# Twelve weight halves on GpSimd, one ring of five buffers, and new transfer figures in the planner of an attention and maxout kernel

## The chip, the core and the metric

The kernel runs on one core of a Trainium2 chip. Its engines are named as in the profile: PE multiplies matrices, DVE, ACT and POOL (GpSimd) work elementwise, SP issues most transfers. The metric is the device time of one execution in microseconds (us); lower is better.

## What is computed

Causal attention over 8 batches of 8 heads (576 positions, head size 64) with a bias from cumulative sums, then an expert layer with three up projections, their maximum, and one down projection, over all 4608 tokens of width 512 (inner width 768).

```python
scores = scale * np.matmul(q, k.transpose(0, 1, 3, 2))
cum = np.cumsum(np.maximum(s, 0.0), axis=-1)
bias = -(cum[:, :, :, None] - cum[:, :, None, :])
scores = np.where(causal, -1000000000.0, scores + np.minimum(bias, 0.0))
attn = softmax(scores)
x = (attn @ v).transpose(0, 2, 1, 3).reshape(B * S, H * D)
h = np.maximum(np.maximum(x @ w1, x @ w2), x @ w3)
out = h @ w_out
```

## The kernel before

**Who sets the order.** The kernel writes no fixed order. It adds each piece of work to a list with `add`: on which engines it may run, with planned durations in ns, a priority key, what it reads and writes. The class `Plan` then runs a small model of the five queues (SP, POOL, DVE, ACT, PE): at each moment each free engine takes the ready piece with the lowest key, and an operation that two engines can do goes to the one that takes it first. The instructions are written out in that order, and each engine of the chip executes its own queue in order. So a changed planned duration costs nothing itself; it moves rows. `load` (L316) plans a transfer with its issue time, bytes by rate, and a latency until it has landed.

**Buffers.** Each kind of buffer is a ring with a depth from the table at L248. A new use of a ring of n waits until the n-th last use has been read by all its readers. Those that matter here: `m`, three PSUM buffers for results of PE; `m1`, three SBUF buffers for the running maximum of the up projections; `o`, two for the outputs on their way to memory.

**Weights.** There are 24 weight tiles of 128 x 512 elements, `w0` to `w17` for the up projections and `w18` to `w23` for the down projection, loaded as eight-byte numbers (`raw`, or `early` for some) in seven groups: three tiles each for up, all six together for down. ACT (L485), POOL (L499, `top`) and DVE (L506, `join`) turn each into fp32. PE forms a small gram block of the group (L527), DVE reduces it (L540) into `ws`, and `power` spreads the largest value over all partitions: a DVE scaling (L425), one matrix multiplication (L434, "m<-identb,ws" in the profile), a DVE maximum (L442). From it come scales: `sws` (L547 to L557), for the down group `rels` (L577). With the scale ready, the high half of a tile is written in fp16 by ACT (L599; POOL has an alternative at L603, for tiles in the range HIP), and the low half, what fp16 left over, by DVE (L637). `power` is used for the values' scales `vs` too.

**Attention.** Scores (`s`, L1149, and L1030 for pairs), masks on POOL (L1222), DVE and ACT for the softmax (L1235, L1244, L1280, L1288), transposes of the probabilities by DMA issued from SP (L1299, L1107, L1116) or for the first units on PE (turns, L1324, copied to `pT` at L1334 and L1336), then probabilities by values (`av`, L1384), whose results become `x` (L1411 to L1429).

**The expert layer.** The tokens go in 16 sets, one of 256 and one of 320 positions in each batch. Set 0 is computed in plain fp32 (`u_plain` L659, `d_plain` L689), while the scales of the weights aren't all there; it needs only raw weights. Sets 1 to 15 use the fp16 halves, three products for each: 18 up blocks `u` of 12 matrix multiplications (L1479), and four down blocks `d` of 18 (L1535). The first of three up blocks is copied from PSUM into `m1` (L1490 on ACT, L1494 on DVE), the other two are folded in by DVE's maximum (L1502); ACT writes the high half `h` (L1509), POOL its low half (L1514), the last reader of that `m1`. Each `d` block is scaled into an `o` buffer by ACT (L1554), and SP issues its transfer to memory (L1560). A set of the middle stretch of the program is worked beside the attention of the next; at the end only expert sets are left.

Of the kernel before, what the change touches and what calls it, by code (L numbers as in the profile page):

```python
# [71 lines left out]
class Plan:  # L72
# [48 lines left out]
    def run(self):  # L121
# [16 lines left out]
        while left:  # L138
# [4 lines left out]
            while events and events[0][0] <= now:  # L143
                _, _, _, op = heapq.heappop(events)
                if op is not None and op.start is None:
                    op.due = now + HOLD[0]
                    for e in op.ways:
                        heapq.heappush(wait[e], (op.key, op.n, op))
            for e in engines:
                if free[e] > now:  # L150
                    continue
                aside, pick, kept = [], None, None
                while wait[e]:
# [16 lines left out]
                if pick is None:  # L170
                    pick = kept
# [8 lines left out]
                if len(op.ways[e]) > 2:  # L180
                    dma[e] = max(dma[e], now + busy) + op.ways[e][2]
# [32 lines left out]
def kernel(  # L214
# [34 lines left out]
        qr=2, qh=2, ql=2, rv=4, vv=2, bias=2, p=2, pr=2, tl=2, pT0=2, pT1=2, tT=2, t=5, m1=3, o=2,  # L249
        sc=6, dg=2, am=3, vs=5, ws=3, os=4, s=2, av=1, m=3,  # L250
# [113 lines left out]
    def spans(c0, c1):  # L364
# [56 lines left out]
    def power(t, key):  # L421


        def do(e):
# [20 lines left out]


# [14 lines left out]

    def weights(c):
        ids = chunks[c]
        raw = {}
# [126 lines left out]
        for i in ids:  # L591
# [51 lines left out]

    def first_set(c, raw):
# [4 lines left out]
        if c < NFT:  # L649
# [3 lines left out]
            for i in range(3):  # L653
                pm = buf("m", free=True, name=f"u_plain_{c}_{i}")
                r = raw[3 * c + i]

                def up(e, r=r, pm=pm):
                    for kt in range(NKT):
                        nc.tensor.matmul(  # L659
                            pm()[:, :nq], lhsT=words(r)[0][:, kt * P:(kt + 1) * P], rhs=xb()[:, kt * nq:(kt + 1) * nq],  # L660
# [967 lines left out]
```

## Time and profile before

| what | value |
|---|---|
| median of three runs | 785.98 us (785.86 to 788.97) |
| the profiled execution | 784.61 us, span 782.6 us |
| PE busy | 764.8 us, 98% of the span |
| DVE, ACT, POOL busy | 573.8, 519.2, 308.3 us |
| moved to and from memory | 75.64 MB read, 9.58 MB written |

The span runs from the first to the last instruction that the profiler recorded; 2.0 us of the execution lie around it. An engine's busy time counts its own instructions. PEld are the weight loads of PE, which overlap its multiplications. In a timeline row stand the start, the duration, the engine, the line of the program and what is written from what; a bracket at its end gives how long the engine stood idle before it and which instruction or transfer ended that. The profile numbers buffers of one kind alike: "o" is any output buffer, "m" any of the small PSUM results.

### The profile page before, as it was taken

What the parts mean: (1) busy time and instruction counts of PE and PEld (TensorE: products, weight loads), DVE (VectorE), ACT (ScalarE), POOL (GpSimd) and SP (SyncE); (2) the same over time, 40 slices, a digit from 0 to 9 for tenths busy, and PEclk for the clock granted to TensorE, in tenths of its full rate; (3) what the DMA queues carried; (4) which work ended last, traced back from release to release, by engine and by line L of the source; (5) the groups of instructions that cost most, each with busy time, mean ns of one, the idle gap of its engine ahead of it and who ended that gap; (6) DMA issues with size and microseconds to landing.
All of it is one profiled execution on the core that took longest, in us unless ns stands there. A gap on an engine that the chain in (4) does not pass through costs nothing. (4 is left out here: it accounts for less than half of the span.)

```text
span 782.6 us, 19630 instructions
## 1 busy us (share of the span) xinstructions
PE 764.8 (98%) x7189; PEld 589.6 (75%) x7189; DVE 573.8 (73%) x1691; ACT 519.2 (66%) x1369; POOL 308.3 (39%) x361
## 2 busy tenths in 40 slices
PE   7889999999999999999999899999999999999998
PEld 5677888888888877766788677667776777778875
DVE  6999898875587888888878787888787977322131
ACT  6878777871687787986887777777876977111101
POOL 4432423641355455444544364354444452011110
PEclk9999999999999999999999999999999999999999
DMA  9799778890399899998999999898989865300000
GB/s 342 245 260 242 180 169 164 176 237 18 97 207 233 199 175 214 227 215 200 225 232 207 183 192 240 241 190 198 254 210 169 208 137 100 81 1 34 28 2 34
DMA packets 241167, 136.31 MB, mean 174 GB/s; under 512 B 204080, under 2 KB 222000, under 8 KB 241072
## 3 DMA queue, kind: packets, MB, share of 16 engines
q1 hardware_dynamic: 240912, 134.78, 75.7%
q8 instruction: 56, 0.92, 0.5%
q14 instruction: 39, 0.32, 0.2%
q10 hardware_dynamic: 160, 0.30, 0.1%
HBM read 75.64 MB, written 9.58 MB: 109 GB/s over the span
## 5 line engine op out<-in xcount | busy, mean ns | idle before, releaser
L1479 PE MATMUL u<-x,w 128*128 128x320 f16 (+1 forms) x3240 | 411.3, 287 | 2.9 <-ACT o L1554 2.9
L1479 PEld LDWEIGHTS <-w 128*128 128x128 f16 x3240 | 312.6, 98 | 99.5 <-issue 17.6
L1514 POOL TENSOR_TENSOR h<-m,h 128x320 f16<-128x320 f32 (+1 forms) x90 | 69.9, 777 | 190.4 <-ACT h L1509 174.5
L1535 PE MATMUL d<-h,w 128*128 128x320 f16 (+1 forms) x1080 | 137.9, 287 | 0.1
L1502 DVE SCALAR_TENSOR_TENSOR m<-u,m 128x320 f32<-128x320 f32 (+1 forms) x180 | 82.2, 457 | 64.3 <-PE u L1479 60.1
L1535 PEld LDWEIGHTS <-w 128*128 128x128 f16 x1080 | 104.7, 98 | 30.4 <-issue 3.2
L1222 POOL TENSOR_SCALAR_AFFINE_SELECT p<-bias 128x256 f32<-128x256 f32 (+3 forms) x91 | 68.9, 770 | 120.6 <-DVE pr L1288 68.9
L1244 ACT ACTIVATE p<-p,sc 128x256 f32<-128x256 f32 (+3 forms) x182 | 98.2, 540 | 26.3 <-DVE sc L1235 25.6
L1509 ACT ACTIVATE h<-m 128x320 f16<-128x320 f32 (+1 forms) x90 | 39.4, 438 | 102.9 <-DVE m L1502 102.6
L1288 DVE SCALAR_TENSOR_TENSOR pr<-p,sc,pr 128x256 f16<-128x256 f32 (+3 forms) x182 | 100.3, 567 | 8.0 <-ACT pr L1280 7.8
L1280 ACT ACTIVATE pr<-p,sc 128x256 f16<-128x256 f32 (+3 forms) x182 | 89.3, 538 | 13.0 <-DMA pT<-pr 7.9
L961 POOL TENSOR_TENSOR ql<-qr,qh 128x256 fp32r<-128x256 f32 (+1 forms) x76 | 82.5, 1106 | 35.0 <-ACT qh L949 30.6
L1235 DVE CUSTOM_DVE_ANT_0 p<-s,p 128x256 f32<-128x256 f32 (+3 forms) x182 | 80.4, 467 | 3.7 <-POOL p L1222 2.2
L1384 PEld LDWEIGHTS <-vv 128*64 128x64 f16 x1232 | 58.6, 110 | 18.1 <-issue 10.0
L1384 PE MATMUL av<-pT,vv 128*64 128x320 f16 (+3 forms) x1104 | 70.3, 276 | 1.2 <-DVE x L1429 0.8
L1494 DVE TENSOR_SCALAR m<-u 128x320 f32<-128x320 f32 (+1 forms) x55 | 25.3, 461 | 48.2 <-PE u L1479 47.6
L1554 ACT ACTIVATE o<-d,os 128x320 f32<-128x320 f32 (+1 forms) x60 | 28.2, 498 | 47.6 <-PE d L1535 36.8
L766 DVE TENSOR_REDUCE am<-rv 128x1 f32<-128x640 f32 (+1 forms) x44 | 33.9, 777 | 13.2 <-DMA rv<-in_qkv_dram 13.0
L1222 POOL TENSOR_SCALAR_AFFINE_SELECT ha<-bias 128x1024 f32<-128x1024 f32 (+3 forms) x29 | 26.7, 926 | 41.8 <-DVE r L1288 29.8
L1244 ACT ACTIVATE ha<-ha,sc 128x512 f32<-128x512 f32 (+3 forms) x58 | 35.9, 620 | 6.5 <-DVE sc L1235 6.1
L815 DVE SCALAR_TENSOR_TENSOR vv<-rv,vs,vv 128x640 f16<-128x640 f32 (+1 forms) x44 | 39.0, 887 | 0.4
L1288 DVE SCALAR_TENSOR_TENSOR r<-ha,sc,r 128x512 f16<-128x512 f32 (+3 forms) x58 | 37.5, 660 | 2.3 <-ACT r L1280 2.2
(170 smaller groups left out, 980.1 us busy)
## 6 DMA issues: line engine op xcount, KB each, us to landing
bias<-cd SPq DMA_DIRECT2D x32, 576.0 KB, 5.0
qr<-in_qkv_dram SPq DMA_DIRECT2D x28, 480.0 KB, 5.2
rv<-in_qkv_dram SPq DMA_DIRECT2D x32, 320.0 KB, 3.8
raw<-in_w_dram SPq DMA_DIRECT2D x16, 512.0 KB, 5.7
qr<-in_qkv_dram SPq DMA_DIRECT2D x13, 512.0 KB, 6.3
bias<-cd SPq DMA_DIRECT2D x12, 512.0 KB, 5.4
out_dram<-o SPq DMA_DIRECT2D x32, 160.0 KB, 2.4
early<-in_w_dram SPq DMA_DIRECT2D x8, 512.0 KB, 7.0
```

What stands on the lines that cost most here:

```text
L961: lambda e, d0=d0, d1=d1: E[e].tensor_tensor(out=lo().bitcast(F32R)[:, d0:d1], in0=raw()[:, d0:d1], in1=hi()[:, d0:d1], op=ALU.subtract),
L1222: nc.gpsimd.affine_select(out=pt()[:, 0:8 * P].rearrange("p (j n) -> p j n", j=2)[:, :, at:at + nk], in_=r["bias"]()[:, 2 * a * w:2 * (a + ...
L1235: lambda e, j=j: nc.vector.tensor_tensor_reduce(out=pj(j), in0=src(j), in1=pj(j) if masked else bias(j), scale=-SCALE, scalar=3.0e38, op0= ...
L1244: lambda e, j=j: nc.scalar.activation(out=pj(j), in_=pj(j), func=AF.Exp, scale=-1.0, bias=nm()[:, j:j + 1], accum_out=sm()[:, j:j + 1]),
L1280: lambda e, h_=h_, s_=s_, j=j: nc.scalar.activation(out=h_(), in_=s_(), func=AF.Copy, scale=ri()[:, j:j + 1]),
L1288: lambda e, h_=h_, l_=l_, s_=s_, j=j: nc.vector.scalar_tensor_tensor(out=l_(), in0=s_(), scalar=ri()[:, j:j + 1], in1=h_(), op0=ALU.mult, ...
L1384: nc.tensor.matmul(av()[j * D:(j + 1) * D, c0:nq], lhsT=lt, rhs=rt, start=(n < 2), stop=(n >= len(todo) - 2), skip_group_check=True,)
L1479: nc.tensor.matmul(pm()[:, :nq], lhsT=v[:, wt, kt, :], rhs=x(xt, kt), start=(k == 0), stop=(k == 3 * NKT - 1),)
L1502: lambda e, pm=pm, m1=m1: nc.vector.scalar_tensor_tensor(out=m1()[:, :nq], in0=pm()[:, :nq], scalar=HSC, in1=m1()[:, :nq], op0=ALU.mult, o ...
L1509: lambda e, m1=m1, ft=ft: nc.scalar.activation(out=h(0, ft), in_=m1()[:, :nq], func=AF.Copy),
L1514: lambda e, m1=m1, ft=ft: E[e].tensor_tensor(out=h(1, ft), in0=m1()[:, :nq], in1=h(0, ft), op=ALU.subtract),
L1535: nc.tensor.matmul(pm()[:, :nq], lhsT=v[:, wt, dt, :], rhs=h(c, ft), start=(k == 0), stop=(k == 3 * NFT - 1), skip_group_check=True,)
```

## The change

Four things change at the constants that are set (many other lines of the diff are switches that are off, or move the down part of a set into the function `down_all` as it was).

1. HIP goes from (0, 0) to (12, 24): the high halves of tiles 12 to 23 are planned on POOL alone (1300 ns), with the tensor_scalar that was there before, and no longer on ACT.
2. The rings `m1` of three and `o` of two become one ring `m1` of five; outputs take their buffers from it. The memory used is the same.
3. The figures of transfers change: a rate, a time from issue to the start of the transfer (`lead`, which takes the place of the issue time there), shorter issue times for some, and a latency with a reserve of 1500 ns on top (SPARE). The planned time of the matrix multiplication in `power` falls from 250 to 90 ns, that of the turns from 350 to 270.
4. The rule by which PE's queue is picked is written anew, with a limit on how many pieces are held back; the number of held pieces is 2.

```diff
-HOLD = (3000.0, 30000.0)
+HOLD = (3000.0, 30000.0, 2)
+SAME = 0
+SPARE = 1500.0
-HIP = (0, 0)
+HIP = (12, 24)
...
-                aside, pick, kept = [], None, None
+                aside, pick, kept = [], None, []
...
-                    if kept is not None and op.mode:
-                        break
-                    if e == "PE" and op.mode and not shape and op.due > now > HOLD[1]:
-                        kept = op
+                    if e == "PE" and op.mode:
+                        kept.append(op)
+                        if shape and (op.mode == shape or not SAME):
+                            pick = op
+                            break
+                        if not shape and (len(kept) >= (HOLD2 if now > HOLD2[1] else HOLD)[2] or not op.due > now > HOLD[1]):
+                            pick = kept[0]
+                            break
                         continue
-                    pick = op
+                    pick = kept[0] if kept and shape else op
                     break
...
-                    dma[e] = max(dma[e], now + busy) + op.ways[e][2]
+                    dma[e] = max(dma[e], now + op.ways[e][3]) + op.ways[e][2]
...
-        qr=2, qh=2, ql=2, rv=4, vv=2, bias=2, p=2, pr=2, tl=2, pT0=2, pT1=2, tT=2, t=5, m1=3, o=2,
-        sc=6, dg=2, am=3, vs=5, ws=3, os=4, s=2, av=1, m=3,
+        qr=2, qh=2, ql=2, rv=4, vv=2, bias=2, p=2, pr=2, tl=2, pT0=2, pT1=2, tT=2, t=5, m1=5,
+        sc=6, far=1, dg=2, am=3, vs=5, ws=3, os=4, s=2, av=1, m=3,
...
-    def load(emit, key, nbytes, reads=(), writes=(), queue="SP", rate=0.3, lat=2000.0, begin=0.0):
-        plan.add({queue: (lat, 450.0, nbytes / rate * 1e-3)}, emit, key, reads, writes).ready = begin
+    def load(emit, key, nbytes, reads=(), writes=(), queue="SP", rate=0.36, lat=1285.0, begin=0.0, lead=1440.0):
+        plan.add({queue: (lat + SPARE, 400.0, nbytes / rate * 1e-3, lead)}, emit, key, reads, writes).ready = begin
...
-            {"PE": (250.0, 250.0)},
+            {"PE": (250.0, 90.0)},
...
-            o = buf("o", free=True, name=f"o_plain_{dt}")
+            o = buf("m1", free=True, name=f"o_plain_{dt}")
...
-            load(spread, k - LOOK[2], 4 * P * nb_ * rows_, [cd], [bias], lat=4500.0 if u < 4 else 2500.0)
+            load(spread, k - LOOK[2], 4 * P * nb_ * rows_, [cd], [bias], lat=3000.0 if u < 4 else 1065.0, rate=0.266, lead=1590.0)
...
-        tw = lambda n: (2000.0, 1250.0, 200.0 * n)
+        tw = lambda n: (1570.0 + SPARE, 1200.0 if n < 10 else 1450.0 if n < 14 else 2000.0, 156.0 * n, 545.0)
...
-            add({"PE": (350.0 * (qb + 1) + 80.0, 350.0 * (qb + 1))}, turn, t, [(pt, (qb, j)), (pr, (qb, j))], [(m, j)])
+            add({"PE": (270.0 * (qb + 1) + 80.0, 270.0 * (qb + 1))}, turn, t, [(pt, (qb, j)), (pr, (qb, j))], [(m, j)])
...
-            o = buf("o", free=True, name=f"o{n}_{dt}")
+            o = buf("m1", free=True, name=f"o{n}_{dt}")
...
-                FIRST, 4 * P * nq, [o], lat=1500.0,
+                FIRST, 4 * P * nq, [o], lat=1320.0, lead=120.0, rate=0.45,
```

Since the planner sees other durations and another ring, the order of every engine changes. PE has 12419 rows in both; of the operations that two engines can do, 28 in place of 35 first maxima now go to ACT (L1490) and 62 in place of 55 to DVE (L1494). In the changed program the same code stands at other line numbers; each fence says which are which. Three places follow.

**The outputs of set 8, ACT and SP.** On ACT before: `o_0` to `o_3` are the four outputs of the set, `pr` and `r` probabilities, `p` and `ha` scores, and `m_0` the first maximum of the next set.

```order
L1554 ACTIVATE o_0_7462<-d_0_7399,os_5157 128x256
L1554 ACTIVATE o_1_7481<-d_1_7424,os_5157 128x256
L1280 ACTIVATE r_7486<-ha_7243,sc_7394 128x4x128 x2
L1244 ACTIVATE p_7451,sc_7512<-p_7451,sc_7512 128x384 x2
L1252 ACTIVATE sc_7512<-sc_7512 128x2
L1244 ACTIVATE p_7488,sc_7519<-p_7488,sc_7519 128x512
L1280 ACTIVATE pr_7550<-p_7451,sc_7512 128x3x128 x2
L1244 ACTIVATE p_7488,sc_7519<-p_7488,sc_7519 128x512
L1252 ACTIVATE sc_7519<-sc_7519 128x2
L1554 ACTIVATE o_2_7574<-d_2_7493,os_5157 128x256
L1554 ACTIVATE o_3_7587<-d_3_7521,os_5157 128x256
L1490 ACTIVATE m_0_7590<-u_0_0_7553 128x320
```

On ACT in the change (L1583 is the old L1554, L1345 the old L1244, L1381 the old L1280):

```order
L1583 ACTIVATE o_0_7469<-d_0_7397,os_5099 128x256
L1381 ACTIVATE r_7474<-ha_7243,sc_7374 128x4x128 x2
L1583 ACTIVATE o_1_7505<-d_1_7421,os_5099 128x256
L1345 ACTIVATE p_7476,sc_7507<-p_7476,sc_7507 128x384 x2
L1583 ACTIVATE o_2_7538<-d_2_7486,os_5099 128x256
L1353 ACTIVATE sc_7507<-sc_7507 128x2
L1345 ACTIVATE p_7510,sc_7540<-p_7510,sc_7540 128x512
L1381 ACTIVATE pr_7553<-p_7476,sc_7507 128x3x128
L1583 ACTIVATE o_3_7569<-d_3_7519,os_5099 128x256
L1381 ACTIVATE pr_7553<-p_7476,sc_7507 128x3x128
```

The third and fourth output come earlier among the scores, and the first maximum of the next set no longer stands on ACT behind them. On SP before, with transposes into `pT` and `tT`, loads of `rv` and `bias`, and the outputs' transfers:

```order
L1116 DMA_TRANSPOSE tT_0_7420<-tl_0_7319 128x1x128
L753 DMA rv_7444<-in_qkv_dram 128x640
L1116 DMA_TRANSPOSE tT_1_7448<-tl_1_7321 128x1x128
L753 DMA rv_7479<-in_qkv_dram 128x640
L1560 DMA out_dram<-o_0_7462 128x256
L1560 DMA out_dram<-o_1_7481 128x256
L1299 DMA_TRANSPOSE pT_29_3_7396<-pr_7441 128x12x128
L1299 DMA_TRANSPOSE pT_29_3_7396<-r_7486 128x16x128
L878 DMA bias_7571<-cd 128x1152
```

On SP in the change (L1589 is the old L1560, L1400 the old L1299):

```order
L1217 DMA_TRANSPOSE tT_0_7439<-tl_0_7319 128x1x128
L851 DMA rv_7446<-in_qkv_dram 128x640
L851 DMA rv_7453<-in_qkv_dram 128x640
L1217 DMA_TRANSPOSE tT_1_7472<-tl_1_7321 128x1x128
L1589 DMA out_dram<-o_0_7469 128x256
L1400 DMA_TRANSPOSE pT_29_3_7415<-pr_7441 128x12x128
L1589 DMA out_dram<-o_1_7505 128x256
L1589 DMA out_dram<-o_2_7538 128x256
L1400 DMA_TRANSPOSE pT_29_3_7415<-r_7474 128x16x128
L1589 DMA out_dram<-o_3_7569 128x256
```

The transfers of the four outputs stand one by one between transposes, where before they stood two by two. On PE the three blocks `u_0_0` to `u_0_2` of the next set now stand ahead of the score pair of L1030, with a small `m` of `power` among them; before, one stood ahead and two behind.

**The scale of the second weight group, DVE.** Before, from the reduction of the gram block to its use:

```order
L540 TENSOR_REDUCE ws_575<-m_518 128x1
L637 SCALAR_TENSOR_TENSOR w_568<-raw_179,sws,w_568 128x512
L1336 COPY pT_1_3_584<-m_573 128x256
L637 SCALAR_TENSOR_TENSOR w_571<-raw_190,sws,w_571 128x512
L425 TENSOR_SCALAR ws_575<-ws_575 128x1
L637 SCALAR_TENSOR_TENSOR w_579<-raw_194,sws,w_579 128x512
L442 TENSOR_REDUCE ws_575<-m_595 128x1
```

In the change (L582, L439, L456 are the old L540, L425, L442; L1437 is the old L1336, L679 the old L637, L1514 the old L1413):

```order
L582 TENSOR_REDUCE ws_582<-m_517 128x1
L439 TENSOR_SCALAR ws_582<-ws_582 128x1
L916 SCALAR_TENSOR_TENSOR vv_573<-rv_203,vs_430,vv_573 128x512
L456 TENSOR_REDUCE ws_582<-m_588 128x1
L589 TENSOR_SCALAR rts<-ws_582 128x1
L595 RECIPROCAL sws<-rts 128x1
L864 TENSOR_REDUCE am_608<-rv_401 128x1
L1437 COPY pT_1_3_515<-m_590 128x512
L599 TENSOR_SCALAR sws<-sws 128x1
L604 TENSOR_SCALAR rts<-rts 128x1
L1336 ISA p_595,sc_624<-s_410,p_595 128x128
L1336 ISA sc_624 128x1
```

The next rows of the change are two score passes, the low half of `w_585`, and the copy of `av_3_0` into `x_0`, the last that `u_plain` needs. The two low halves and the copy that stood between the reduction and the scaling have moved behind the scales.

**The down group's high halves, POOL and ACT.** Before, ACT had them, right behind the scale:

```order
L810 ACTIVATE vv_1865<-rv_625,vs_747 128x512
L599 ACTIVATE w_1880<-early_160,rels 128x512
L599 ACTIVATE w_1897<-raw_1351,rels 128x512
L599 ACTIVATE w_1905<-raw_1367,rels 128x512
L599 ACTIVATE w_1909<-raw_1473,rels 128x512
L599 ACTIVATE w_1912<-raw_1497,rels 128x512
L701 ACTIVATE o_plain_1930<-d_plain_1882 128x256
L599 ACTIVATE w_1942<-early_160,rels 128x512
L1422 ACTIVATE x_0_1608<-av_2_0_1917 128x256
```

In the change POOL has them (L645 is the old L603), between masks `p` for scores (L1323), and ahead of the split of the next query tile into `ql`:

```order
L1323 AFFINE_SELECT p_1918<-bias_1232 128x2x128
L1323 AFFINE_SELECT p_1918<-bias_1232 128x2x256
L645 TENSOR_SCALAR w_2009<-early_160,rels 128x512
L645 TENSOR_SCALAR w_2050<-raw_1314,rels 128x512
L645 TENSOR_SCALAR w_2068<-raw_1333,rels 128x512
L645 TENSOR_SCALAR w_2079<-raw_1572,rels 128x512
L645 TENSOR_SCALAR w_2094<-raw_1591,rels 128x512
L645 TENSOR_SCALAR w_2102<-early_160,rels 128x512
L1062 TENSOR_TENSOR ql_2132<-qr_1974,qh_2090 128x512
L1323 AFFINE_SELECT p_2153<-bias_1617 128x2x128
L1323 AFFINE_SELECT p_2153<-bias_1617 128x2x256
```

On PE, between the `m` of `power` for this group and the first block `d` of set 1, there stand in the change three plain d blocks, one av, two s and one u block; before, there stood two plain d blocks, another `m`, an av, two s, one more plain d block and four u blocks.

More of the change, by code (lines that the diff above doesn't have):

```diff
@@ L30 @@
 FAST = 8
-HOLD = (3000.0, 30000.0)
+HOLD = (3000.0, 30000.0, 2)
+SAME = 0
+D16 = 0
+SPARE = 1500.0
+FAR = 99
+AMK = 6.0
+H16K = 20.0
+KP = 0
+HOLD2 = (3000.0, 900.0e3, 2)
 M01 = (0, 99)
 NDB = 0
-HIP = (0, 0)
+HIP = (12, 24)
 RAW0 = 6
@@ L40 @@
 P3 = 10
+RAWX = 0
+LATE = 0.0
 LOWP = (2, 24)
@@ L145, in run @@
                 if op is not None and op.start is None:
-                    op.due = now + HOLD[0]
+                    op.due = now + (HOLD2 if now > HOLD2[1] else HOLD)[0]
                     for e in op.ways:
@@ L169, in run @@
                     heapq.heappush(wait[e], it)
-                if pick is None:
-                    pick = kept
+                if pick is None and kept:
+                    pick = kept[0]
                 if pick is None:
@@ L336 @@
     cct = inner("cc", 12 * S, 4 * S)
-    load(lambda e: E[e].dma_start(out=st()[0:HB], in_=s), -1000.0, 4 * HB * S, writes=[st], queue="ACT")
+    load(lambda e: E[e].dma_start(out=st()[0:HB], in_=s), -1000.0, 4 * HB * S, writes=[st], queue="ACT", lat=2000.0)
     def do(e):
@@ L400 @@
     load(
-        lambda e: E[e].dma_start(out=cd(), in_=cct()[0:HB]), -1000.0, 4 * HB * S, [cct], [cd], queue="ACT", lat=5500.0
+        lambda e: E[e].dma_start(out=cd(), in_=cct()[0:HB]), -1000.0, 4 * HB * S, [cct], [cd], queue="ACT", lat=4000.0
     )
@@ L443, in power, with far_power @@
             key, [gm], [(t, 2)],
+        )
+    def far_power(t, key, n):
+        fd = Buf(plan, f"far{n}", lambda b: dram.tile([P, 1], F32, name=f"far{n}"), "one")
+        row = buf("far", name=f"far_row{n}")
+        add(
+            {"DVE": (157.0, 75.0)},
+            lambda e: nc.vector.tensor_scalar(
+                out=t()[:, 1:2], in0=t()[:, 0:1], scalar1=2.0 ** -80, scalar2=1.0 / VSC, op0=ALU.max, op1=ALU.mult
+            ),
+            key, [(t, 0)], [(t, 1)],
+        )
+        load(lambda e: E[e].dma_start(out=fd(), in_=t()[:, 1:2]), key, 4 * P, [(t, 1)], [fd], rate=1.0e-3)
+        load(
+            lambda e: E[e].dma_start(out=row(), in_=fd().rearrange("p o -> o p").to_broadcast([P, P])),
+            key, 4 * P * P, [fd], [row],
+        )
+        add(
+            {"DVE": (282.0, 200.0)},
+            lambda e: nc.vector.tensor_reduce(out=t()[:, 2:3], in_=row(), axis=AX.X, op=ALU.max),
+            key, [row], [(t, 2)],
         )
@@ L466, in weights @@
             k = (i if i < RAW else i - 1) % RAW
-            if i == RAW:
+            if RAWX:
+                k = RAWAT[i]
+            if RAWX and i > RAW and k < 0:
+                r = buf("ql" if k == -1 else "qh", name=f"raw{i}")
+            elif i == RAW:
                 r = Buf(plan, "r6", lambda b: early3()[:, 0:2 * N], "one", inside=early3)
@@ L595, in weights @@
             r = raw[i]
-            k = wkey(i)
+            k = wkey(i) + LATE
             add(
@@ L683, in first_set @@
         hb = H0[0]
+        if D16:
+            split_first(hb)
+            return
         for dt in range(NDT):
@@ L755, in values_in @@
         sk = (b, kind)
-        if plain(u):
+        if plain(u) and not D16:
             return
@@ L768, in values_in @@
             ),
-            k - 4.0, [rv], [(am, col)],
+            AMK if plain(u) else k - 4.0, [rv], [(am, col)],
         )
@@ L772, in values_in @@
             vs = VS[sk] = buf("vs")
-            kk = begin[u] - (1.0 if kind == "split" else 4.0)
+            kk = AMK if plain(u) else begin[u] - (1.0 if kind == "split" else 4.0)
             add(
@@ L778, in values_in @@
             )
-            power(vs, kk)
+            if u >= FAR:
+                far_power(vs, kk - 1.0, u)
+            else:
+                power(vs, kk)
             add(
@@ L1518, in experts @@
             )
[L1519 to L1562 removed]
+        down_all(n, t0, nq, hb, h, vs, base)
     gone = 0
```

165 lines of the change are left out of this document (108 added, 57 removed).

## The prediction

> **What bounds the kernel now.** The page comes first: which engine is busy almost all the time.
>
> ```profile
> span 782.6 us, 19630 instructions
> PE 764.8 (98%) x7189; PEld 589.6 (75%) x7189; DVE 573.8 (73%) x1691; ACT 519.2 (66%) x1369; POOL 308.3 (39%) x361
> ```
>
> PE is busy for 764.8 of 782.6 us, so 17.8 us of the span is PE standing still. The change leaves every matrix multiplication as it is; only that idle time can be won. Where it lies is read from the busy time by stretches (columns: stretch, length, busy us of PE, PEld, DVE, ACT and POOL, then clock, DMA share, GB/s).
>
> ```profile
> 0.00:20.00 20.00, 16.01 (x145) 10.64 (x145) 14.03 (x58) 13.95 (x45) 9.07 (x22) 1.00 0.95 343
> 20.00:60.00 40.00, 35.59 (x362) 28.74 (x361) 38.83 (x154) 33.37 (x102) 15.92 (x22) 1.00 0.95 253
> 60.00:120.00 60.00, 57.93 (x647) 49.46 (x645) 52.30 (x175) 45.21 (x125) 19.41 (x28) 1.00 0.80 186
> 120.00:440.00 320.00, 319.89 (x3124) 256.18 (x3119) 255.39 (x752) 239.84 (x643) 147.00 (x167) 1.00 0.87 190
> 440.00:520.00 80.00, 76.81 (x691) 54.37 (x690) 63.94 (x164) 57.74 (x136) 37.59 (x38) 1.00 0.98 212
> 520.00:740.00 220.00, 219.31 (x1950) 162.20 (x1949) 140.41 (x376) 123.81 (x311) 74.53 (x80) 1.00 0.60 135
> 740.00:782.60 42.60, 39.22 (x289) 28.02 (x287) 8.85 (x18) 5.29 (x11) 4.75 (x6) 1.00 0.06 19
> ```
>
> Length less PE's busy time gives 3.99 + 4.41 + 2.07 = 10.5 us idle in the first 120 us, 0.1 in the next 320, 3.2 from 440 to 520, 0.7 up to 740, and 3.4 at the end (the closing output). The clock is 1.00 everywhere. What PE waited for there is in its waits (sum in us, times, longest).
>
> ```profile
> PE u L1479 <- ACT o L1554: 2.9, 2, 2.1
> PE m L434 <- ACT o L1554: 0.3, 1, 0.3
> ```
>
> So there are two separate accounts: the start, where PE mostly waits for short DVE operations (DVE is busy for 38.83 of the 40 us from 20 to 60), and the middle, where it waits for the eviction of the outputs, o.
>
> **The ring of five.** The timeline of PE, ACT and SP at the worst place (start, duration):
>
> ```profile
> 434.87 0.84 ACT L1554 ACTIVATE o<-d,os 128x256 f32<-128x256 f32 x2
> 440.45 1.79 PE L1479 MATMUL u<-x,w 128*128 128x320 f16 x12
> 440.51 0.86 SPq L1560 DMA_DIRECT2D out_dram<-o x2
> 444.97 0.84 ACT L1554 ACTIVATE o<-d,os 128x256 f32<-128x256 f32 x2 [3.65 <-DMA out_dram<-o]
> 445.49 3.42 PE L1479 MATMUL u<-x,w 128*128 128x320 f16 x24 [2.11 <-ACT o L1554]
> ```
>
> The chain reads backwards: u waits for a PSUM buffer that d still holds; d is held because ACT has no o buffer; both o buffers wait for transfers that SP issued 5.6 us after the eviction at 434.87, as it stood behind transposes. With five shared buffers the third and fourth output need no landed transfer: they take buffers last used by maxima that POOL has long read. The waits on o's line, 2.9 and 0.3, are **3.2 us**, all there is from 440 to 520. The same merging can cost: the next set's second maximum takes the first output's buffer. Counted from the eviction at 434.87, PE has the rest of d until 440.45, then three u blocks of 1.7 (3.42 for two) and further work, and that maximum begins with the end of a fourth: 5.6 + 4 x 1.7 = 12.4 us later at least, while the transfer was issued after 5.6 and takes
>
> ```profile
> out_dram<-o SPq DMA_DIRECT2D x4, 128.0 KB, 4.2
> ```
>
> 4.2 us in that window (its DMA issues): landed after 9.8. I take −3.0; bounds −3.2 and 0.
>
> **Recorded transfer times.** The old plan counts a 512 KB load as 0.45 + 1.75 + 2.0 = 4.2 us; the page has 5.7 for weight tiles, and the new figures make 1.44 + 1.46 + 2.79 = 5.7. The row of the page (KB, us to landing):
>
> ```profile
> raw<-in_w_dram SPq DMA_DIRECT2D x16, 512.0 KB, 5.7
> ```
>
> What came late for PE in the middle is small: of the 0.7 us idle from 520 to 740 half may go; but the new order of every engine can put a new gap anywhere. I take −0.3, bounds −0.7 and +1.0. Since SP issues in order, nothing else is queued behind a longer planned time: the number only moves rows.
>
> **The start.** One stall there is 1.75 us, and the timelines of DVE and PE show why:
>
> ```profile
> 19.07 0.67 DVE L766 TENSOR_REDUCE am<-rv 128x1 f32<-128x512 f32 x1
> 24.83 1.60 PE L1324 MATMUL m<-pr-2_481,p-2_427 128*128 128x128 f32 x12
> 26.16 0.18 DVE L540 TENSOR_REDUCE ws<-m 128x1 f32<-128x32 f32 x1
> 26.26 0.79 DVE L637 SCALAR_TENSOR_TENSOR w<-raw,sws,w 128x512 f16<-128x512 f32 x1
> 26.97 0.41 DVE L1336 COPY pT<-m 128x256 f32<-128x256 f32 x1
> 27.30 0.77 DVE L637 SCALAR_TENSOR_TENSOR w<-raw,sws,w 128x512 f16<-128x512 f32 x1
> 27.99 0.14 DVE L425 TENSOR_SCALAR ws<-ws 128x1 bf16<-128x1 f32 x1
> 28.19 0.23 PE L434 MATMUL m<-identb,ws 128*128 128x128 bf16 x1 [1.75 <-DVE ws L425]
> 29.20 0.87 PE L1384 MATMUL av<-pT,rv 128*64 128x256 f32 x8
> 30.01 3.30 PE L659 MATMUL u_plain<-x,raw 128*128 128x256 f32 x14
> ```
>
> Three DVE operations stand between the reduction and the scale, 0.79 + 0.41 + 0.77 = 1.97 us; in the changed order none does. But they don't vanish: the next thing PE needs is the first x, and in the changed order DVE now has, between that matrix multiplication and the last copy of x, one split of v, a reduction of rv (0.67), a copy of pT of 512 columns (about as long), two short score passes, one low half (0.79) and the copy of x (as long as the 0.41 of 256 columns). The four with a figure are 2.5 us, with the score passes about 3.1, and PE has 1.9 beside them (two thirds of the twelve turns of 1.60, and an av of 0.87): a new stall of 1.2 us or more ahead of u_plain in place of 1.75, since the split and small steps come on top. DVE's queue up to that point holds the same work, so u_plain starts at 30.0 ± 0.7 either way: **nothing** here. The stalls behind it come from loads that landed late and from scales behind long operations; the planner now knows the late landing, so I take −1.0 for them of
>
> ```profile
> PE av L1384 <- DVE x L1429: 0.8, 1, 0.8
> PE u_plain L659 <- PE m L434: 0.9, 1, 0.9
> PE m L434 <- DVE vs L425: 1.0, 2, 0.6
> ```
>
> 2.7 us. For the start as a whole the bounds are −4 and +2: the order is new, and a scale at the wrong place costs 1.75.
>
> **The high halves on POOL.** Twelve operations leave ACT for POOL, where no row shows this form. The nearest rows:
>
> ```profile
> L599 ACT ACTIVATE w<-raw,rels x4: 737/745/753, 104.5 to 106.4; 128x512 f16<-128x512 f32 x4
> L499 POOL TENSOR_SCALAR raw<-raw x14: 657/689/1193, 12.2 to 87.7; 128x512 int32<-128x512 uint32 x14
> L961 POOL TENSOR_TENSOR ql<-qr,qh x76: 724/1274/1856, 115.9 to 625.9; 128x512 fp32r<-128x512 f32 x48, 128x256 fp32r<-128x256 f32 x28
> ```
>
> From 0.69 (one input, same size) to 1.86 (the longest with two inputs); I take 0.78 for it, near the one-input row, while the plan has 1.30. ACT gets 12 x 0.75 = 9 us back, but ACT isn't what PE waits for at 60 to 110 us, so that is worth nothing. What may be lost is at the first d, where all six tiles of the last group are needed:
>
> ```profile
> 99.98 0.23 PE L434 MATMUL m<-identb,ws 128*128 128x128 bf16 x1 [0.56 <-DVE ws L425]
> 100.54 1.89 PE L689 MATMUL d_plain<-h_plain,raw 128*128 128x256 f32 x8
> 103.80 0.77 ACT L599 ACTIVATE w<-early,rels 128x512 f16<-128x512 f32 x1 [2.60 <-DVE rels L577]
> 106.24 0.69 PE L1384 MATMUL av<-pT,vv 128*64 128x256 f16 x12
> 108.22 0.71 PE L689 MATMUL d_plain<-h_plain,early 128*128 128x256 f32 x2
> 110.92 5.40 PE L1479 MATMUL u<-x,w 128*128 128x256 f16 x48
> ```
>
> In the changed order PE has between that scale and d three plain d blocks (twelve passes each, about 2.7), an av and two s (2.0, from 106.24 to 108.22) and one u block (a quarter of 5.40), about 11.4 us. The scales take 3.8 (99.98 to 103.80), then five operations of d us and one low half of 0.8: PE would wait 5d − 6.8. At 0.78 nothing (2.9 us to spare), at the planned 1.30 nothing (0.3), at 1.86 a wait of 2.5. I take 0, bounds 0 and +2.5.
>
> **A rule that speaks against it.** The row of L499 runs from 657 to 1193 ns for one form and size, so something stretches POOL's work at times; by its worst, d = 1.19 and the wait is still nothing. The Trainium skill ("GPSIMD Engine Reference", 4.1 Engine selection) gives elementwise work to VectorE, since GpSimd takes about twice as long with two inputs and is at roughly line rate with one. Its section 1 adds that GpSimd shares the SBUF interfaces with VectorE and contends with DVE instructions that have two SBUF inputs, as L637 does. The spread of L499 fits that, though the trace doesn't show its cause; what such a stretch would do here is rival 3, and by the rows without it the sum stays as it is.
>
> **The sum.** −3.0 (ring) −0.3 (transfers) −1.0 (start) + 0 (POOL) = −4.3 us. The profiled execution took 784.61 (span 782.6 and 2.0 around it), so 780.3 on its scale; it was 1.4 below the median of the runs, 785.98. On the median's scale: **781.7**.
>
> **Rivals.** What a measurement of this kernel can tell from no change is about 0.5%, 3.9 us, so the forecast lies just at that border.
> 1. *The start gains more.* For it: 10.5 us idle, all of it behind short waits; against: DVE at 38.83 of 40. With −4 there: 785.98 − 7.3 = 778.7; chance 0.18.
> 2. *New waits take the place of the old.* Every queue is reordered; if three new gaps of about 1 us appear, the size of most rows of the waits above, 784.7; chance 0.27.
> 3. *Slower: POOL sets the first d.* Six of these stand in one row on POOL while DVE follows with the low halves. If that stretched them to 2.6, twice the planned price, PE would wait 5 x 2.6 − 6.8 = 6.2: 787.9. From d = (6.8 + 4.3)/5 = 2.2 on the gain is eaten. Against it: no row of these lines is that long, 1.86 is the longest. Chance 0.06, a third of it beyond 0.5%.
> 4. *Slower: outputs hold the maxima's buffers.* SP issues in order; if an output lands over 12.4 us after its eviction, the second maximum waits, then PSUM, then PE, at up to 14 set ends: each us beyond is worth up to 14. Half a us gives 788.7 with the other gains, more than 790 from 0.6 on. Against it: 9.8 at the worst place seen. Chance 0.07.
> 5. *Nothing happens.* The changed rule for picking PE's work acts as the old one with these constants, and the rest only reorders: 786; chance 0.04.
>
> The forecast itself, 780 to 783.5, has 0.38, of which 0.28 lies below 782.05. **Faster** by over 0.5%: 0.28 + 0.18 = 0.46; **slower** by over 0.5%: 0.02 + 0.07 = 0.09; the rest, 0.45, is **within** 0.5%. The range: from 785.98 − (3.2 + 0.7 + 4) = 778.1, less 0.6, about half of what the profiled execution and the median differ by, to 787.5, which takes in rivals 2 and 5 and most of 3 and leaves out about 0.15.
>
> **What would show it.** Right: no wait of u on L1554's o (now another line) near 445 and 500, under 1 us idle from 120 to 740; POOL's new row near 0.7 to 0.8 us; first u_plain at 30 with a wait for x of 1 to 2 ahead of it; d of set 1 without a wait. Wrong: a wait of m on outputs, ACT or DVE waiting for DMA out_dram before a maximum, a wait of PE on DVE's low halves near 110, or first 120 us with more than 10.5 us idle.

## The result, and the profile after

The changed kernel is slower: 796.06 us, median of four runs (794.89 to 799.32), against 785.92 for the kernel before; the ratio is 1.0126 (95% interval 1.0087 to 1.0164). The ratios here leave out disturbed executions, so a ratio need not be that of two medians. The profiled execution took 795.79 us, its span 794.0. The page's first lines:

```profile
span 794.0 us, 19639 instructions
PE 769.1 (97%) x7189; PEld 591.2 (74%) x7189; DVE 584.4 (74%) x1699; ACT 509.2 (64%) x1349; POOL 332.4 (42%) x373
```

The span grew by 11.4 us. PE's idle time (span less busy time) grew from 17.8 to 24.9, which is 7.1; the other 4.3 are PE being busy longer with the same work. The stretches of before, now of the changed kernel (columns as there):

```profile
0.00:20.00 20.00, 12.82 (x60) 7.79 (x61) 8.84 (x33) 8.21 (x27) 5.86 (x15) 0.78 0.93 328
20.00:60.00 40.00, 36.15 (x419) 29.63 (x418) 39.06 (x149) 35.88 (x112) 16.74 (x25) 0.98 0.78 223
60.00:120.00 60.00, 56.72 (x647) 47.55 (x636) 56.83 (x198) 37.68 (x111) 34.70 (x37) 1.00 0.88 204
120.00:440.00 320.00, 318.02 (x3076) 253.58 (x3075) 251.15 (x730) 232.08 (x625) 149.58 (x168) 1.00 0.84 186
440.00:520.00 80.00, 77.45 (x711) 56.06 (x709) 64.88 (x166) 57.71 (x139) 37.70 (x37) 1.00 0.95 202
520.00:740.00 220.00, 217.40 (x1915) 158.43 (x1913) 153.35 (x406) 130.21 (x324) 81.76 (x85) 1.00 0.68 144
```

Three things stand in them. In the first 20 us PE did 60 recorded matrix multiplications in place of 145, at a granted clock of 0.78 in place of 1.00; over the first 120 us it stood idle for 14.3 us in place of 10.5. From 60 to 120 us DVE is busy 56.8 in place of 52.3, and POOL 34.7 in place of 19.4. And the middle didn't get clean: 2.6 us idle from 440 to 520 (3.2 before), 2.6 from 520 to 740 (0.7 before), 2.0 from 120 to 440 (0.1 before). PE's waits name the places (sum in us, times, longest):

```profile
PE s-2_291 L1250 <- DVE sc L1336: 4.3, 1, 4.3
PE m L448 <- DVE vs L439: 4.3, 4, 1.9
```

No wait of u for an output is left: the forecast gain of the ring was had, and paid out again, mostly by waits for the values' scale `vs` (L439 is the old L425), 1.9 us at 456 and 1.6 at 616.

**The start.** ACT's timeline shows what held it: the issue of cd, a small transfer of bias data that ACT itself starts.

```profile
8.56 0.58 ACT L1027 ACTIVATE bias<-m 128x512 f32<-128x512 f32 x1
13.90 0.48 ACTq L415 DMA_DIRECT2D cd<-early  x1
14.43 0.66 ACT L527 ACTIVATE early<-raw 128x512 f32<-128x512 f32 x1 [5.28 <-DMA rv<-in_qkv_dram]
```

In the kernel before the same issue stood ahead of the bias copies, at 7.60. Now it stands behind the first of them and isn't issued until 13.90, when a load of rv has landed, though cd has nothing to do with rv. The waits in the two programs tell why. A semaphore is a counter that a transfer raises when it has landed. The transfers of this kernel take eight of them, DMAHW0 to DMAHW7, in turn, and each issue waits until the transfer before it on the same semaphore, eight issues back, has landed.

```
before, ACT: L401 DMA cd<-early 64x576 [waits DMAHW2_49,DVE_49]
change, ACT: L415 DMA cd<-early 64x576 [waits DMAHW0_49,DVE_49]
change, SP:  L842 DMA rv_198<-in_qkv_dram 128x2x256 [waits DMAHW0_49]
change, SP:  L519 DMA early_160<-in_w_dram 128x512 [waits DMAHW1_49]
```

In the new order cd's issue is the eighth behind that of the first rv load, so it fell on that load's semaphore, and the load was issued at 5.08 only; before, it had that of a query load issued at 1.18. The traces' own records agree: in the change cd's issue and that rv load carry the same semaphore number, and ACT's wait for it ends at 13.84. Everything behind the issue on ACT waited too: the second bias copy, then POOL's mask, DVE's score pass, and PE. The clock followed (stretches of 2 us):

```profile
10.00:12.00 2.00, 0.87 (x6) 0.47 (x7) 1.29 (x8) 0.00 (x0) 0.70 (x2) 0.81 1.03 400
12.00:14.00 2.00, 1.22 (x8) 0.49 (x6) 0.00 (x0) 0.00 (x0) 0.00 (x0) 0.50 1.05 385
20.00:22.00 2.00, 2.00 (x12) 1.95 (x12) 1.46 (x7) 2.00 (x6) 1.07 (x2) 0.63 0.89 223
```

PE ran at half clock from about 11.2 to 21.5 us. The first u_plain (now L743) began at 36.75, against 30.01 before:

```profile
35.95 0.87 PE L1485 MATMUL av<-pT,rv 128*64 128x256 f32 x8 [1.56 <-DVE rts L604]
36.75 3.51 PE L743 MATMUL u_plain<-x,raw 128*128 128x256 f32 x15
```

**The high halves** on POOL, and the low halves that DVE makes beside them (min/median/max in ns):

```profile
L645 POOL TENSOR_SCALAR w<-raw,sws x4: 1590/1602/2044, 77.5 to 91.8; 128x512 f16<-128x512 f32 x4
L645 POOL TENSOR_SCALAR w<-raw,rels x4: 1591/1609/1616, 117.5 to 122.2; 128x512 f16<-128x512 f32 x4
L679 DVE SCALAR_TENSOR_TENSOR w<-raw,rels,w x4: 860/1132/1217, 119.5 to 123.9; 128x512 f16<-128x512 f32 x4
```

1.6 us in place of the 0.75 on ACT, and the low halves 1.13 in place of 0.74. That the move stretches the low halves shows in hip_back below, the change with the high halves on ACT: 0.742. It doesn't explain all of DVE's longer time from 60 to 120 us, for DVE is busy 56.2 us there in hip_back too: most of that is the new order.

### The profile page after: what moved, and what is told of

Its sections match the earlier page's. It is cut to its first block, busy times and chain, and to the rows that moved or that the text cites. A ratio compares the mean times of both kernels' runs of the same rounds, so it can differ in the third digit from the quotient of the medians.

```text
span 794.0 us, 19639 instructions
## 1 busy us (share of the span) xinstructions
PE 769.1 (97%) x7189; PEld 591.2 (74%) x7189; DVE 584.4 (74%) x1699; ACT 509.2 (64%) x1349; POOL 332.4 (42%) x373
## 4 chain that ended last, share of the span: by engine, by line
PE 66%; DVE 12%; DMA 9%; ACT 6%; issue 4%; POOL 2%; SPq 0%; POOLq 0%; DVEq 0%; ACTq 0%
PE u L1627 38%; PE d L1564 13%; PE av L1485 5%; PE s L1250 5%; DMA rv<-in_qkv_dram 3%; DMA qr<-in_qkv_dram 3%; PE s L1131 2%; DVE p L1336 2%; DMA pT<-pr 2%; POOL w L645 2%; DVE w L679 1%; DVE m L1650 1%; PE u_plain L743 1%; ACT pr L1381 1%; DVE pr L1389 1%
## 5 line engine op out<-in xcount | busy, mean ns | idle before, releaser
L1323 POOL TENSOR_SCALAR_AFFINE_SELECT p<-bias 128x256 f32<-128x256 f32 (+3 forms) x91 | 71.7, 798 | 117.2 <-DVE pr L1389 51.9
L1381 ACT ACTIVATE pr<-p,sc 128x256 f16<-128x256 f32 (+3 forms) x182 | 89.2, 539 | 33.0 <-DVE sc L1363 17.5
L1389 DVE SCALAR_TENSOR_TENSOR pr<-p,sc,pr 128x256 f16<-128x256 f32 (+3 forms) x182 | 104.6, 590 | 5.8 <-ACT pr L1381 5.7
L1345 ACT ACTIVATE p<-p,sc 128x256 f32<-128x256 f32 (+3 forms) x182 | 97.8, 539 | 15.5 <-DVE sc L1336 14.8
L1336 DVE CUSTOM_DVE_ANT_0 p<-s,p 128x256 f32<-128x256 f32 (+3 forms) x182 | 80.4, 465 | 3.0 <-POOL p L1323 1.4
L1485 PEld LDWEIGHTS <-vv 128*64 128x64 f16 x1232 | 58.8, 110 | 17.8 <-issue 9.8
L1642 DVE TENSOR_SCALAR m<-u 128x320 f32<-128x320 f32 (+1 forms) x62 | 28.1, 454 | 49.0 <-PE u L1627 48.8
L1583 ACT ACTIVATE o<-d,os 128x320 f32<-128x320 f32 (+1 forms) x60 | 28.3, 495 | 33.5 <-PE d L1564 28.5
L1323 POOL TENSOR_SCALAR_AFFINE_SELECT ha<-bias 128x1024 f32<-128x1024 f32 (+3 forms) x29 | 26.8, 928 | 43.6 <-DVE r L1389 20.9
L1050 ACT ACTIVATE qh<-qr 128x896 fp32r<-128x896 f32 (+1 forms) x40 | 38.9, 972 | 9.0 <-DMA qr<-in_qkv_dram 8.6
L864 DVE TENSOR_REDUCE am<-rv 128x1 f32<-128x640 f32 (+1 forms) x44 | 33.6, 774 | 13.2 <-DMA rv<-in_qkv_dram 13.1
L1381 ACT ACTIVATE r<-ha,sc 128x512 f16<-128x512 f32 (+3 forms) x58 | 33.1, 620 | 11.7 <-DMA pT<-r 5.4
```

The source lines that it names most:

```text
L1323: nc.gpsimd.affine_select(out=pt()[:, 0:8 * P].rearrange("p (j n) -> p j n", j=2)[:, :, at:at + nk], in_=r["bias"]()[:, 2 * a * w:2 * (a + ...
L1336: lambda e, j=j: nc.vector.tensor_tensor_reduce(out=pj(j), in0=src(j), in1=pj(j) if masked else bias(j), scale=-SCALE, scalar=3.0e38, op0= ...
L1345: lambda e, j=j: nc.scalar.activation(out=pj(j), in_=pj(j), func=AF.Exp, scale=-1.0, bias=nm()[:, j:j + 1], accum_out=sm()[:, j:j + 1]),
L1381: lambda e, h_=h_, s_=s_, j=j: nc.scalar.activation(out=h_(), in_=s_(), func=AF.Copy, scale=ri()[:, j:j + 1]),
L1389: lambda e, h_=h_, l_=l_, s_=s_, j=j: nc.vector.scalar_tensor_tensor(out=l_(), in0=s_(), scalar=ri()[:, j:j + 1], in1=h_(), op0=ALU.mult, ...
L1485: nc.tensor.matmul(av()[j * D:(j + 1) * D, c0:nq], lhsT=lt, rhs=rt, start=(n < 2), stop=(n >= len(todo) - 2), skip_group_check=True,)
```

## The experiments

Three theories came out of this. S: the held issue at the start. P: the price of the high halves on POOL. O: the order that ring and figures make in the middle. Each kernel was timed beside the kernel before; the ratios are to that.

| kernel | what it is | ratio, 95% interval |
|---|---|---|
| the change | all | 1.0126 (1.0087 to 1.0164) |
| cd_first | change, cd issued first | 1.0084 (1.0052 to 1.0115) |
| act_held | before, ACT held | 1.0078 (1.0048 to 1.0108) |
| hip_back | change, HIP (0, 0) | 1.0105 (1.0075 to 1.0135) |
| cd_first_hip_back | change, both | 1.0021 (0.9998 to 1.0044) |
| hip_only | before, HIP (12, 24) | 1.0028 (1.0010 to 1.0047) |
| figures_cd_first | figures alone, cd first | 1.0020 (1.0003 to 1.0036) |
| ring_only | before, ring of five | 1.0011 (0.9991 to 1.0030) |
| ring_rv | ring, rv at 4.5 us | 0.9973 (0.9948 to 0.9997) |
| ring_rv6 | ring, rv at 6.0 us | 0.9955 (0.9934 to 0.9976) |
| ring_rv75 | ring, rv at 7.5 us | 0.9976 (0.9956 to 0.9996) |
| hip_two | hip_only, two operations | 1.0003 (0.9979 to 1.0026) |
| cd_first_two | cd_first, two operations | 1.0033 (1.0009 to 1.0056) |

**The start: cd_first and act_held.** cd's issue is moved in the finished order, right behind the DVE operation that makes its data:

```diff
     plan.run()
+    up = plan.seq.index(next(o for o, w, _ in cct.log if w))
+    plan.seq.remove(cd.ops[0])
+    plan.seq.insert(up + 1, cd.ops[0])
     plan.write()
```

> The changed kernel with one difference: the issue of the transfer cd on ACT stands right behind the DVE operation that makes its data, ahead of ACT's first bias copy, as in the kernel before. Theory S (the start: ACT's queue is held 5.3 us by that issue, which waits for the landing of a load of rv, and PE's clock falls to 0.5 meanwhile): first u_plain at 30 to 31 us in place of 36.8, clock 1.00 throughout, 788 to 790.5 us. Theory P (what costs is the price of the high halves on POOL, 1.6 us each): the start is caught up later, 794 to 796.

792.52 us. ACT issues cd at 7.68 and runs through; u_plain begins at 31.57. Theory S holds for the start, but a third of the loss came back (4.2 of 12.6 thousandths) and not the half or more that it expected. Part of the reason may be the clock, which in this profile fell to 0.50 once more, from 30.6 to 34.1 us; the one of the four executions with a mean clock of 1.000 took 788.91. act_held goes the other way, into the kernel before:

```diff
...
+    hold.emit = lambda e: nc.scalar.activation(out=warm(), in_=rv0()[:, 0:1], func=AF.Copy)
+    plan.seq.insert(at + 1, hold)
     plan.write()
```

> The kernel before with one operation more: right behind its first bias copy ACT copies one column of the first loaded rv into the scratch column warm, and so waits for that load's landing at the place where the changed kernel waits. Theory S: ACT idle some 4 to 5 us there, the clock falls to 0.5 for some 10 us, 791 to 793 us. Theory P: a late start is covered by what comes after, 786 to 787.

791.19 us, and ACT's row:

```profile
14.30 0.20 ACT L1583 ACTIVATE warm<-rv 128x1 f32<-128x1 f32 x1 [4.95 <-DMA rv<-in_qkv_dram]
```

A wait of 4.95 us on ACT at this place costs 0.0078, some 6 us, its effect on the clock included; nothing behind it makes that good. Here too u_plain begins at 36.6, and the clock is 0.50 from 16.0 to 22.8 us and again from 36.5 to 39.9. So the held issue accounts for between a third (cd_first) and two thirds of the change's loss (act_held, and the two repairs together below). It wasn't tried to keep cd's place on ACT and change its semaphore alone; that the wait is for the semaphore rests on the list of waits, on the semaphore numbers in the trace and on the load that ended it.

**The high halves: hip_back, cd_first_hip_back, hip_only.**

```diff
-HIP = (12, 24)
+HIP = (0, 0)
```

> The changed kernel with HIP back at (0, 0): all high halves on ACT, rings and figures as changed. Theory S: the start keeps its wait, 793.5 to 796 us. Theory P: 790 or less.

> The changed kernel with both differences of the earlier runs: cd's issue on ACT ahead of the first bias copy, and HIP back at (0, 0). If the two costs are separate, what each run won adds up: 796.1 - 3.5 - 3.2 = 789.4 us, and 788 to 790 with the clock at 1.00 from the start. If they cover each other (a late start hides POOL's price), 791 or more.

> The kernel before with HIP = (12, 24) and nothing else. Theory P: POOL takes 1.6 us for a high half here too, DVE's low halves beside them take 1.1 us in place of 0.74, and 788 to 790 us. Rival (its price shows only because the late start left no cover): within 1 us of 786.

hip_back: 792.86 us, just below what theory S expected: with the late start left in, most of the loss stays. Both together: 788.17, a ratio of 1.0021 whose interval just takes in 1, though in this profile the clock was 0.50 from 13.1 to 19.9 us and u_plain began at 33.67. With the issue repaired, taking HIP back is worth 0.0063, some 5 us, give or take 3. HIP alone in the kernel before costs 0.0028, some 2 us, between its two expectations, with the same 1.6 us on POOL: PE's idle time from 60 to 120 us rises from 2.1 to 3.7. Most of the rise is one wait, of the first d for a maximum that stands on DVE behind the low halves:

```profile
119.93 3.54 PE L1535 MATMUL d<-h,w 128*128 128x256 f16 x31 [1.37 <-DVE m L1494]
```

**What makes it 1.6 us: prices and prices2.** Two tails, operations added behind the last work of the kernel before, time forms on POOL by themselves.

> The kernel before with a tail behind its last work, in which POOL does six groups of four operations of 128 x 512 on buffers that are no longer needed, so its time is longer by that tail: the high half's form (fp32 words eight bytes apart, scale from SBUF, fp16 out); the same with adjacent words; the same as the first with fp32 out; as the first with a constant scale; as that with fp32 out; and the first again while DVE does its low half's form. If contention with DVE made the 1.6 us: near 0.7 alone, 1.6 beside DVE. If the scale from SBUF makes it: 1.6 wherever the scale is from SBUF and 0.7 with a constant. If the fp16 output makes it: 1.6 with fp16, 0.7 with fp32.

Adjacent words, fp32 out or a constant scale changed nothing, 1.51 to 1.60 without DVE beside it. So none of the three guesses held: the form takes 1.6 us alone, and beside DVE it took 1.58 to 1.92. The second tail:

> The kernel before with another tail on POOL, four operations of 128 x 512 of each form: the high half's form (fp32 in, scale from SBUF, one operation, fp16 out); fp32 in, two constants (multiply, add), fp16 out; uint32 in, two constants, fp16 out; L499's form (uint32 in, int32 out, two constants, in place); and that with one operation. L499 took 0.66 to 0.69 in the kernel before, the high half's form 1.59. If the single operation makes it slow: 0.7 for every form with two, 1.6 for those with one. If the fp32 input makes it: 1.6 for the first two, 0.7 for the three with integers. If the conversion between types makes it: 0.7 for none but L499's form.

```profile
L1586 POOL TENSOR_SCALAR w<-x,sws x4: 1592/1596/1612, 776.2 to 781.3; 128x512 f16<-128x512 f32 x4
L1588 POOL TENSOR_SCALAR w<-x x4: 637/640/646, 783.0 to 785.2; 128x512 f16<-128x512 f32 x4
L1594 POOL TENSOR_SCALAR x<-x x4: 638/639/639, 788.8 to 790.9; 128x512 int32<-128x512 uint32 x4
L1598 POOL TENSOR_SCALAR x<-x x4: 1531/1531/1531, 791.6 to 796.5; 128x512 int32<-128x512 uint32 x4
```

The first and the last have one operation, the two between them two (multiply, then add). With a second operation POOL's tensor_scalar is 2.4 to 2.5 times as fast, for fp32 and for integers. L499, the row that the prediction leaned on, has two; the high half has one.

**The remedy in the kernel: hip_two and cd_first_two.**

```diff
-                    out=w()[:, 0], in0=words(r)[0], scalar1=sc(), scalar2=None, op0=ALU.mult
+                    out=w()[:, 0], in0=words(r)[0], scalar1=sc(), scalar2=0.0, op0=ALU.mult, op1=ALU.add
```

> The kernel before with HIP = (12, 24) as in the earlier run, and a second operation (add 0.0) in POOL's tensor_scalar for the high half; the same order. If the single operation was what made POOL's high halves long, also with the scale from SBUF: 0.65 to 0.8 us each, DVE's low halves near 0.74, no wait for the high halves, 785 to 786.5 us. If the scale from SBUF alone keeps them at 1.6: 787 to 788 again.

> The changed kernel with cd's issue first and the same second operation in POOL's high half; otherwise as changed, HIP at (12, 24). If the start and POOL's price are the two costs that matter: as with HIP taken back, 786.5 to 789 us. If twelve operations more on POOL cost by their place in its queue whatever they take: 790 to 793, as with cd first alone.

hip_two: 785.1 us, ratio 1.0003; the second operation helps with the scale from SBUF too, though less than in the tail:

```profile
L603 POOL TENSOR_SCALAR w<-raw,sws x4: 726/982/1298, 72.5 to 79.8; 128x512 f16<-128x512 f32 x4
L603 POOL TENSOR_SCALAR w<-raw,rels x4: 734/958/1177, 108.3 to 110.9; 128x512 f16<-128x512 f32 x4
```

They took 0.73 to 1.30 us, and the four of the `early` tiles up to 1.67, in place of the 0.65 to 0.8 that were expected. What stretches them wasn't taken apart; DVE's low halves run beside them. The order is that of hip_only, and the first d now hardly waits:

```profile
117.47 3.55 PE L1535 MATMUL d<-h,w 128*128 128x256 f16 x31 [0.21 <-DVE m L1494]
```

cd_first_two: 788.45, ratio 1.0033, in the range of the first expectation, so it is the price and not the place in POOL's queue that cost. At that price the moved work costs nothing that can be seen in the kernel before, and brings nothing either: ACT wasn't waited for.

**The middle: figures_cd_first, ring_only and ring_rv.**

> The transfer figures, the planned times of power and turns and the rewritten rule of PE alone: the changed kernel with HIP at (0, 0), the rings as before (m1 three, o two), and cd's issue first. If the figures cost only through cd's place: 785 to 787 us. If their order also makes PE wait for scales of v or outputs in the middle: 788 or more.

787.49 us, 1.0020: between the two expectations. In its profile PE waits 2.7 us once for vs, and 2.3 once for an output (rings as before).

> The kernel before with the rings m1 and o merged into one of five and nothing else. Theory O (the ring does what it was forecast to do, and the new figures' order gives it back): no wait of u on an output near 445 and 500, 782 to 784 us. Rival (the ring itself makes new waits of maxima for outputs): 786 or more.

786.53 us, 1.0011: the rival's range, but not by the rival's mechanism. No u waits for an output and no maximum for a transfer; PE's timeline shows what came in their place:

```profile
454.35 0.23 PE L434 MATMUL m<-identb,vs 128*128 128x128 bf16 x1 [0.96 <-DVE vs L425]
555.47 0.23 PE L434 MATMUL m<-identb,vs 128*128 128x128 bf16 x1 [1.76 <-DVE vs L425]
```

This small matrix multiplication spreads the values' scale. The scale needs the last rv load of the batch, which SP issues behind transposes:

```profile
545.88 3.33 SPq L1116 DMA_TRANSPOSE tT<-tl  x2
552.49 0.82 DVE L766 TENSOR_REDUCE am<-rv 128x1 f32<-128x640 f32 x1 [2.01 <-DMA rv<-in_qkv_dram]
```

For the second of the two waits, two tT transposes hold SP's queue for 3.33 us, the loads go out at 549.30, and DVE waits 2.01 for the first to land. PE's order was written for loads that land when planned. In the kernel before, the wait for o hid such a wait near 445: it took 2.11 us right ahead of the same multiplication, which ran at 448.75 with its scale ready at 447.95, so without it PE would have stood there some 1.3 us for the scale. Near 555 nothing hid it: there the kernel before waits for no output, and SP issued the two loads at 541.45, ahead of the transposes; the order with the ring of five puts them behind. In the change DVE waits for loads of rv in the same way ahead of PE's waits at 456 and 616 (1.35 us, and 1.62 and 1.10). If this is what is left, a later planned landing of these loads alone, in the old figures, moves the small multiplication down PE's queue and leaves nothing:

```diff
-                ... in_=qkv[b, gs[0], :, V0:QKV]), k - LOOK[1], 4 * P * 640, writes=[rv]
+                ... in_=qkv[b, gs[0], :, V0:QKV]), k - LOOK[1], 4 * P * 640, writes=[rv], lat=6000.0
```

> The kernel before with the ring of five, and the planned latency of the loads of rv for the later units at 4.5 us in place of 2.0, so that the small matrix multiplication for the values' scale stands later in PE's order. If the waits for vs took the place of the waits for o: under 1 us idle from 440 to 520, under 1.2 from 520 to 740, 782 to 784 us. Rival (another wait for the same late loads follows at once, av for vv): 785.5 or more.

> The kernel before with the ring of five and the planned latency of the later rv loads at 6.0 us (4.5 in the run before this, which left one wait for vs of 2.9 us at 506): that matrix multiplication stands about one u block later. If nothing new becomes late: under 0.5 us idle from 440 to 740, 781.5 to 784 us. Rival: av or vv waits for the later scale in its place, 784.5 or more.

> As the run before it with 7.5 us planned: the matrix multiplication for vs stands behind the av blocks in most sets. If lateness of the rv loads is all that was left: as with 6.0, 781.5 to 784 us. If the scale is then late for the split of v: waits of av, 785 or more.

ring_rv (4.5 us): 784.5 us, 0.9973, above its 782 to 784; one wait of 2.94 was left at 506. ring_rv6: **782.87 us, 0.9955 (0.9934 to 0.9976)**, faster than both kernels, and the two stretches are full:

```profile
440.00:520.00 80.00, 80.00 (x719) 56.93 (x718) 66.84 (x174) 60.86 (x142) 38.28 (x39) 1.00 0.96 212
520.00:740.00 220.00, 220.00 (x1959) 162.63 (x1958) 142.16 (x380) 125.12 (x313) 74.09 (x80) 1.00 0.60 136
```

The 3.9 us that were idle there before are gone: the 3.2 of the ring term and the 0.7 up to 740. ring_rv75 fills them as well (0.9976, 784.19 us); whether it is really slower than with 6.0 the intervals don't tell. The later landing wasn't tried in the changed kernel.

## Why the prediction was wrong

It said 781.7 (777.5 to 787.5) and gave slower by over 0.5% a chance of 0.09. By its own steps:

1. **Recorded transfer times (term −0.3): the step that failed most.** It held that "nothing else is queued behind a longer planned time: the number only moves rows". The rows moved past another queue: cd's issue on ACT came to stand behind SP's loads, took the semaphore of one that hadn't landed, and ACT's queue stood behind it for 5.3 us. act_held puts such a wait at 0.0078, some 6 us, in place of the −0.3 with its bound of +1.0. The prediction followed SP's queue and not the transfer that ACT issues. The move comes, by elimination, from the new figures or PE's rule: with the high halves back on ACT (hip_back) u_plain still begins at 36.83, and with the ring alone PE does 142 matrix multiplications in the first 20 us, as good as the 145 of before. Which of the figures does it wasn't taken apart.
2. **The start (−1.0, u_plain at 30.0 ± 0.7).** It began at 36.75 for the same reason. The local reading was right: the stall ahead of the small multiplication shrank, and a new wait stood ahead of u_plain's x, as an av that waits 1.6 for DVE. With the issue repaired u_plain began at 30.94 in figures_cd_first, with the clock at 1.00, and at 31.57 in cd_first, where the clock fell on the way; without the new figures it began between 30.0 and 31.1 (before, hip_two, ring_rv6, hip_only). So the two waits come near to cancelling, as forecast. The bounds of −4 and +2 had no place for a queue that stops, nor for the clock, which had been 1.00 in every row of before.
3. **The high halves (0, bounds 0 and +2.5): a size.** d was taken as 0.78, from a row with the right size and the wrong form; it measured 1.59 to 2.28. By the prediction's own 5d − 6.8 that gives 1.2 us at the first d. In the change it began without a wait, and 0.5 us came a little later, on a low half; so the 0 for this place came out nearly right by luck, with half the true price. In the kernel before, the first d waits 1.37 us, not for a low half but for a maximum that comes late behind them on DVE, and 0.21 once POOL has two operations; that is over half of hip_only's 2 us. Rival 3 had this mechanism. In the changed kernel with the issue repaired the price is some 5 us, and where they lie is open: cd_first and cd_first_two have one order and spans of 790.8 and 786.1, and of these 4.7 us only 1.5 have come about when PE reaches the scores at 339 in the one and 337.5 in the other, long behind the last high half. The intervals don't tell these 5 us (0.0063, give or take 0.004) clearly from the 2.
4. **The ring (−3.0).** Right in what it removes; what would be late next was missed. The stall at 445 covered a wait for vs, and the order that the ring makes on SP brings another, so ring_only shows 1.0011 in place of −3.0 us. With that wait planned away, the gain is there (0.9955). Rival 4, maxima held by outputs, wasn't seen in any of the runs.
5. **Rival 2** (new waits take the place of the old) was the likeliest of those named and is what happened in the middle; it had the size of about 1 us each right, and left out the start.

Added up, the parts are 0.0078 (start) + 0.0028 (HIP) + 0.0011 (ring) + 0.0020 (figures without the start) = 0.0137, against 0.0126 for all together. That fits, but it is a weak test: the intervals make some 0.004 either way for the sum and for the whole, and all parts but the last were measured in the kernel before.

The Trainium skill's rule ("GPSIMD Engine Reference", 4.1) spoke against the move, for another reason than the one that decided. It has one-input work at roughly line rate; the runs have such work of 128 x 512 at 0.64 us with two operations and at 1.51 to 1.60 with one, so one price can't hold for both.

## What to carry to other kernels

A planner's figures move issues on every queue that starts transfers; after such a change, look at the list of waits of each issue that stands on a compute engine, for it stops the engine's queue until a transfer lands that it doesn't use. Ahead of counting a stall as gain, ask which operand would be late at the same place if it weren't there, and which loads the new order puts behind something long. Take a price from a row of the same form, not only of the same size.

## What the runs showed of the hardware

- **One operation is slower than two.** POOL's tensor_scalar on 128 x 512 took 1.53 us (integers) and 1.60 (fp32 in, fp16 out) with a multiplication alone, and 0.64 with a multiplication and an addition, for both (prices2). Other pairs of operations weren't tried, and why it is so isn't known from these runs.
- **The clock falls in steps, and not in each execution.** The times at 0.50 in the first 60 us come as one, two or three times 3.4 us: 3.4 (cd_first, cd_first_two, ring_only, ring_rv, the second of act_held), 6.8 (act_held, hip_back, cd_first_hip_back), 10.2 (the change). In the changed kernel PE stood idle from 10.43, and its clock was 0.50 from about 11.2 to 21.5; in act_held it fell at 16.0, 3.4 us after PE's last work. In cd_first, ring_only and ring_rv a single step of about 3.4 us at 0.50 follows a stall of 1.55, 1.76 and 1.68 us, of the size of the one that the kernel before had with its clock at 1.00. The Trainium skill ("TensorE: Matmul & The Clock Gate", Part 1) tells of a free-running window of 3.4 us: the length agrees, while a fall 0.8 us after the last work, or behind 1.6 us of idle time, doesn't fit its wording of a whole idle window. By these lengths a step of 3.4 us at half clock costs up to 1.7 us of PE's work, an estimate. The kernel before went from 782.2 to 790.3 us in one series of 22 runs, with mean clocks from 1.000 to 0.991; how much of that spread is these steps wasn't measured.
